# Ordering the QKV projections of a transformer block: values of a chunk inside the next chunk's phase, stores and staged loads placed by modelled times, five block tiles at first, 288 pairs of maxima instead of 296

## The chip, the core and the metric

One core of a Trainium2 chip runs the whole program. The metric is the device time of one launch in microseconds (us), the median of several runs. Engines have short names here: PE is TensorE (matmuls; PEld is its weight load), ACT is ScalarE, DVE is VectorE, POOL is GpSimd, and SP is SyncE, whose queue issues every DMA of the part that changes. Each engine has its own queue of instructions, filled in the order in which the program wrote them; this program writes that order out by hand.

## What is computed

A pre-norm transformer block on one sequence of S = 2048 tokens, width D = 640, 32 heads of 20, in float32:

```python
qkv = layernorm(x) @ wqkv                       # (2048, 640) @ (640, 1920)
p   = softmax(q @ k.T * 20 ** -0.5)             # for each of 32 heads
h   = x + (p @ v) @ wo
out = h + (silu(ln(h) @ w_gate) * (ln(h) @ w_up)) @ w_down     # F = 1728
```

Matmuls on float32 are done as three products of parts: a value is split into a rounded part "hi" and the rest "lo", and hi*hi + lo*hi + hi*lo is summed.

## The kernel before, in words

The program has three stages: the projections (from the start to about 370 us), attention (to about 1520 us), and the output projection and feed-forward part. Only the first stage is rewritten by the change; attention changes by a few instructions.

**Projections.** Tokens come in four chunks of 512 (`NC` = 4). To prepare a chunk its x tiles are loaded (`load_x`), normalised on DVE (`norm`, in small pieces handed out over several steps), and turned by PE (`flip`, five per chunk) into z_hi and z_lo. Then come 10 "blocks" (`query_key`, lines L696 to L705), each the queries or the keys of 128 rows for the chunk's 512 tokens, and 8 "values" (`value`), each 128 tokens by 320 columns. A block is 30 matmuls of half the rows of the array, issued in two halves that run side by side; both kinds are issued at line L498. Before the change the order was fixed per chunk: chunk 0 did ten blocks (the first two together at L715) and then its eight values; chunks 1 and 2 mixed key, query and value and ended with three values; chunk 3 did keys, values, queries. Each entry of this list is a "slot", 18 per chunk, 72 in all.

**A block's way out.** A finished block is split by ACT and DVE or POOL (`keep`: L311, L88, L89) into an "e" tile and stored to DRAM (`qk_d`, line L691) by SP. There are three e tiles in turn: two of their own and one that lies in the values' buffer of attention (the trace calls it `v_stk`; in the last chunk another takes its place, `z_hi`). The flips use the e tiles as scratch too. `keep` doesn't store at once: it puts the store on a list, and the next call of `store`, usually one slot later, issues it (function `store`, L686 to L694). An e tile is written again only when its store has landed.

**Staged maxima.** Attention needs the largest score of each query row before it takes exponentials. Part of these maxima is computed early, inside the projections, to fill PE's gaps: keys and queries of one group of four heads (`g`) and one chunk (`c`) are read back from `qk_d` into a "place" by four DMAs (`stack`, L151, called by `load_items`). Places are quarters of the key buffer of attention (`k_stk`), raw weight tiles that have become free (`raw`), and later the old `z_lo`. For two chunks of keys at once, POOL forms their difference (L376), PE multiplies both (L204), ACT takes a relu (L216) and DVE adds and reduces to the maximum (L210); this makes a "twice" product. A single chunk of keys is folded in half instead (L180, L191, L193), two such products to a "pair". All of it together covers 296 pairs. The rest of the maxima is done in attention (L223, L229), three beside every four scores.

**What sets the order.** A small planner (`Halves`, called `pe`) runs while the program is written: it keeps modelled times of PE's two halves, of ACT, DVE and POOL, and issues a staged product where its model says that its inputs are there and that the engines are free. SP is not modelled before the change: when a group's rows can be loaded is read from a table of slots (`stored_at`), and keys count as loaded 6.5 us (modelled) after the issue.

**Attention** loops over 32 units (a group of four heads by a chunk of queries) with 16 tiles of keys each: four scores (L1225), four exponentials on ACT (L1231), four products with values (L1235).

Of the kernel before, what the change touches and what calls it, by code (L numbers as in the profile page):

```python
# [17 lines left out]
P = 128  # L18
S = 2048
# [28 lines left out]
def tile_block(ctx: ExitStack, tc: tile.TileContext, x, wqkv, wo, wg, wu, wd, out):  # L48
# [111 lines left out]
    def load_queries(u):  # L160

        g, c = divmod(u, NC)
        q = queries[u] = stk.tile([P, 2, CH], F32R, name="q_stk", tag="q_stk", bufs=4)
        stack(q, 0, g, slice(c * CH, (c + 1) * CH))
# [7 lines left out]
    spare = stk.tile([P, 2, CH], F32R, name="q_stk", tag="q_stk", bufs=4)  # L172
# [117 lines left out]
    kept = {}  # L290

    def next_e():
        es.append(es.pop(0))
        if kept.pop(id(es[-1]), 0):
            store()
        return es[-1]

    with tc.tile_pool(name="pa", bufs=2) as pa:
        xs = {}
        zs = {}  # L300
# [3 lines left out]
        def load_x(c):  # L304
            for t in range(c * TPC, (c + 1) * TPC):
                xs[t] = pa.tile([P, D], F32, name="xt", tag="xt", bufs=4)
                nc.sync.dma_start(xs[t], x[t * P : (t + 1) * P, :])
# [9 lines left out]
        slot, returned = [0], []  # L317
# [4 lines left out]
        def stored_at(which, g, c):  # L322

            block = ((g + 1) * GD - 1) // P
            if c == 0:
                return 2 * block + 5
            return 18 * c + 4 + 3 * block + (0 if which else 1)

# [3 lines left out]
        own_places = [None, quarters[0]]  # L332
# [9 lines left out]
        def load_items():  # L342
            for lane, places in lanes:
                while lane:
# [3 lines left out]
                        if slot[0] < LAST_QUARTER or not any(p is k for k in quarters)  # L348
# [4 lines left out]
                    if t is None:  # L353
                        t = raw_tile().rearrange("p a b -> p (a b)")[:, : 2 * CH].rearrange(
                            "p (h n) -> p h n", h=2
                        )
                        fill_ones(t)
                    assert landed[which, g, c] == GD
# [22 lines left out]
        def there(n):  # L381
# [3 lines left out]
            return t is not None and pe.now() >= at + 6.5  # L385
# [3 lines left out]
        def staged_keys(u, kc, ks, q=None, since=0):  # L389
# [18 lines left out]
            def over():  # L408
                for n in ns:
                    users[n] -= 1  # L410
                    if not users[n]:
                        lanes[items[n][6]][1].append(items[n][3])
                if u == 0:
# [23 lines left out]
        for c in (1, 0):  # L437
            for g in range(1, NG, 1 if c else 2):
                if (g, c) == (5, 0):
                    early += third_unit()  # L440
                first = stage(1, g, 1 - c, "plain")
# [17 lines left out]
        def next_pair():  # L459
            load_items()  # L460
            queues = (others, early) if slot[0] >= 18 * (NC - 1) else (early, others)
            return next((queue for queue in queues if queue and queue[0][0]()), None)

        class Halves:
# [5 lines left out]
            def __init__(self):  # L470
                self.t = [0.0, 0.0]
                self.free = dict.fromkeys(("vector", "scalar", "pool"), 0.0)
# [16 lines left out]

            def issue(self, half):  # L490
                job = next(j for j in self.jobs if j["at"][half] < j["n"])
# [66 lines left out]
            def flip(self):  # L558
                for half in range(2):
                    if self.second[half]:  # L560
                        self.finish_second(half)
# [4 lines left out]
                self.use("scalar", 0.48)  # L566
                self.use("pool", 1.3, self.free["scalar"] + 0.1)
                del self.single[0]

# [7 lines left out]
            def wait(self, us):  # L577
                self.t = [self.now() + us] * 2

# [64 lines left out]
        def norm(c):  # L644
# [4 lines left out]
            def apply(t):  # L649
# [5 lines left out]
            zs[c] = (  # L655
                pa.tile([P, ND, CH], F32R, name="z_hi"), pa.tile([P, ND, CH], F32R, name="z_lo")
            )
# [3 lines left out]
                + [(0.6, lambda t=t: apply(t)) for t in range(TPC)]  # L661
            )

        def flip(c, k):
# [7 lines left out]
            split_sbuf(ps, z_hi, z_lo, next_e()[:, 0].bitcast(F32))  # L672
# [10 lines left out]

        stores = []

# [1247 lines left out]
```

## Time and profile before

| | us |
|---|---|
| median of three runs | 2078.84 |
| lowest and highest of them | 2075.09, 2085.61 |
| the profiled execution, whole | 2086.12 |
| its span, first to last instruction | 2084.3 |
| busy in the span: PE | 2037.9 |
| DVE | 1617.8 |
| ACT | 1471.6 |
| POOL | 774.7 |
| mean granted clock of PE | 0.988 of full speed |

The profile is of one execution. "Busy" of PE counts time in which at least one matmul was in the array, so two halves at work and one half at work count the same. A row of the view by windows gives a stretch of the span, its length, the busy time of each engine with the number of its instructions, the mean clock that PE was granted (1.00 is full speed), and the busy share and GB/s of the DMA engines. A row of the chain gives start, length and the piece of work that the end waited for. A row of waits gives the total, the number and the longest.

### The profile page before, as it was taken

The numbers are of one execution on the slowest core, as the hardware profiler recorded it, in microseconds if no ns is written. First come the engines' busy times: TensorE is split into PE (matmuls) and PEld (weight loads), VectorE is DVE, ScalarE is ACT, GpSimd is POOL, SyncE is SP. The second block draws the span as 40 slices with busy tenths as digits, with TensorE's granted clock in tenths as the row PEclk, the third lists the DMA queues.
The fourth block names the chain that finished last, engine by engine and source line by source line (L and its number), as shares of the span: only waits on it lengthen the run. The fifth ranks groups of instructions, "written<-read, shape, count | busy, mean of one in ns | idle before, by whom it ended". The sixth has DMA issues, their size and how long they took to land.

```text
span 2084.3 us, 39077 instructions
## 1 busy us (share of the span) xinstructions
PE 2037.9 (98%) x13656; PEld 1245.0 (60%) x13656; DVE 1617.8 (78%) x3251; ACT 1471.6 (71%) x2941; POOL 774.7 (37%) x1082
## 2 busy tenths in 40 slices
PE   7998999999999999999999999999999999999999
PEld 5887888433333333333333333335588888888888
DVE  6665877888888888888888888885368776676667
ACT  3757888999999989999999999996743222212221
POOL 4433453142425342353432001001145444753556
PEclk9898999899999999999999999999999999999999
DMA  7665665053343432533443113132138755884542
GB/s 223 192 203 150 195 192 170 27 150 111 125 150 121 133 115 97 170 124 126 154 150 120 53 32 95 34 111 64 38 123 293 247 185 173 306 302 156 193 157 95
DMA packets 205292, 305.33 MB, mean 146 GB/s; under 512 B 47640, under 2 KB 82456, under 8 KB 204072
## 3 DMA queue, kind: packets, MB, share of 16 engines
q1 hardware_dynamic: 205000, 302.83, 45.1%
q8 instruction: 109, 1.79, 0.4%
q14 instruction: 87, 0.71, 0.1%
q10 hardware_dynamic: 96, 0.00, 0.0%
HBM read 206.27 MB, written 95.68 MB: 145 GB/s over the span
## 4 chain that ended last, share of the span: by engine, by line
PE 89%; DMA 7%; DVE 1%; issue 1%; POOL 1%; SPq 1%; ACT 1%; POOLq 0%; ACTq 0%; DVEq 0%
PE acc L1235 24%; PE ps_one L1225 16%; PE ps_a L1398 15%; PE ps_max L223 11%; PE ps_b L1492 8%; PE ps_one L498 7%; PE ps_single L204 3%; PE ps_max L963 2%; DMA k_stk<-qk_d 1%; PE ps_b L963 1%; DMA raw<-qk_d 1%; DMA halves<-j_d 1%; DMA q_stk<-qk_d 1%; DMA qk_d<-e 1%; PE ps_single L180 1%
## 5 line engine op out<-in xcount | busy, mean ns | idle before, releaser
L1231 ACT ACTIVATE probs<-ps_one 128x512 f32<-128x512 f32 x2048 | 1057.6, 611 | 66.5 <-PE ps_one L1225 26.3
L229 DVE TENSOR_REDUCE mx<-ps_max 128x1 f32<-128x512 f32 x1456 | 915.7, 684 | 124.9 <-PE ps_max L223 76.4
L1225 PE MATMUL ps_one<-q_stk,k_stk 62*128 62x512 f32 x2048 | 586.5, 432 | 1.0 <-DVE mx L210 1.0
L1235 PE MATMUL acc<-probs,v_stk 128*32 128x512 f32 x4096 | 546.7, 606 | 0.0
L223 PE MATMUL ps_max<-k_stk,q_stk 60*128 60x512 f32 x1456 | 486.1, 440 | 3.4 <-DMA q_stk<-qk_d 3.4
L1225 PEld LDWEIGHTS ps_one<-q_stk,k_stk 62*128 62x128 f32 x2048 | 289.8, 186 | 291.3 <-ACT probs L1231 269.6
L223 PEld LDWEIGHTS ps_max<-k_stk,q_stk 60*128 60x128 f32 x1456 | 241.4, 185 | 169.2 <-DVE mx L229 131.6
L1613 DVE TENSOR_TENSOR tmp<-ps_a,tmp 128x512 f32<-128x512 f32 x208 | 141.1, 689 | 120.2 <-PE ps_a L1398 94.3
L1235 PEld LDWEIGHTS acc<-probs,v_stk 128*32 128x32 f32 x4096 | 80.7, 108 | 180.4 <-issue 172.9
L1492 PE MATMUL ps_b<-halves,yp 128*128 128x320 f32 x1032 | 179.3, 308 | 1.8 <-DMA halves<-j_d 1.2
L1492 PEld LDWEIGHTS ps_b<-halves,yp 128*128 128x128 f32 x1032 | 165.1, 188 | 18.4 <-POOL yp L89 1.5
L1398 PE MATMUL ps_a<-t,units 128*128 128x512 f32 x624 | 162.6, 396 | 0.0
L210 DVE CUSTOM_DVE_ANT_0 q_stk<-ps_single,q_stk 128x512 f32<-128x512 f32 x158 | 105.7, 689 | 50.9 <-ACT q_stk L216 40.1
L1398 PE MATMUL ps_a<-z,units 128*128 128x512 f32 x516 | 133.9, 394 | 0.0
L89 POOL TENSOR_TENSOR yp<-y,yp 128x256 fp32r<-128x256 f32 x96 | 60.3, 628 | 187.8 <-ACT yp L88 187.8
L1398 PEld LDWEIGHTS ps_a<-t,units 128*128 128x128 f32 x624 | 112.6, 188 | 18.6
L240 POOL CAST both<-neg 128x16 fp32r<-128x16 f32 x32 | 6.3, 198 | 309.2 <-DVE neg L236 127.8
L1497 DVE TENSOR_TENSOR h<-ps_b,h 128x320 f32<-128x320 f32 x248 | 109.9, 480 | 7.2 <-PE ps_b L1492 5.7
L498 PE MATMUL ps_one<-z_hi,w_lo 64*128 64x512 f32 x380 | 104.5, 401 | 0.0
L216 ACT ACTIVATE q_stk<-ps_single 128x512 f32<-128x512 f32 x158 | 91.6, 596 | 17.8 <-PE ps_single L204 9.4
L1398 PEld LDWEIGHTS ps_a<-z,units 128*128 128x128 f32 x516 | 93.1, 187 | 16.0
L1270 POOL TENSOR_TENSOR o<-o,rb 128x512 f32<-128x512 f32 x31 | 39.9, 1286 | 164.7 <-DMA q_stk<-qk_d 84.3
(209 smaller groups left out, 3001.4 us busy)
## 6 DMA issues: line engine op xcount, KB each, us to landing
units<-w_d SPq DMA_DIRECT2D x186, 256.0 KB
w_d<-stage SPq DMA_DIRECT2D x106, 256.0 KB
halves<-j_d SPq DMA_DIRECT2D x70, 320.0 KB
k_stk<-qk_d SPq DMA_DIRECT2D x114, 160.0 KB
j_d<-stage SPq DMA_DIRECT2D x42, 320.0 KB
q_stk<-qk_d SPq DMA_DIRECT2D x64, 160.0 KB
k_stk<-qk_d SPq DMA_DIRECT2D x114, 80.0 KB
raw<-qk_d SPq DMA_DIRECT2D x56, 160.0 KB
```

The source lines that it names most:

```text
L210: nc.vector.tensor_tensor_reduce(out=place, in0=pss[1], in1=place, scale=1.0, scalar=LEAST, op0=ALU.add, op1=ALU.max, accum_out=mx[:, b, p ...
L216: nc.scalar.activation(place, pss[0], AF.Relu)
L223: nc.tensor.matmul(ps, queries[u][rows, pair, t * P : (t + 1) * P], keys[u // NC][rows, pair, kc * CH : (kc + 1) * CH], start=True, stop=True,
L229: nc.vector.tensor_reduce(mxs[u][:, b, pair, t, kc : kc + 1], ps, axis=AX.X, op=ALU.max)
L498: product = nc.tensor.matmul(job["ps"][:, :out], lhs, rhs, start=(half == 0 and i == 0), stop=(half == 1 and i == job["n"] - 1),)
L1225: nc.tensor.matmul(ps, keys[u // NC][rows, p, kt * P : (kt + 1) * P], queries[u][rows, p, :], start=True, stop=True,)
L1231: nc.scalar.activation(probs[p][:, b, :], ps, AF.Exp, scale=scale)
L1235: nc.tensor.matmul(acc[32 * j : 32 * j + 32, :], values[u // NC][:, kt, j * VW : j * VW + 32], probs[j // 2][:, j % 2, :], start=(kt == 0) ...
L1398: nc.tensor.matmul(ps.rearrange("p (t n) -> p t n", t=TPC), w[k][:, i], z[k][:, :, j], start=(first and m == 0), stop=(last and m == len(n ...
L1492: nc.tensor.matmul(ps, a, b, start=(n == 0), stop=(n == len(pairs) - 1))
L1497: nc.vector.tensor_tensor(out=h, in0=ps, in1=h, op=ALU.add)
L1613: add = lambda out, ps, x: nc.vector.tensor_tensor(out=out, in0=ps, in1=x, op=ALU.add)
```

## The change

What it does, in the order of the diff:

- The order of slots: ten slots of chunk 0's blocks; then for chunks 1 to 3 a phase of 18 in which two values of the chunk before and two blocks of the chunk alternate, blocks alone at its end; and chunk 3's eight values last. The number of slots stays 72.
- The x tiles of a chunk become one tile with one buffer; flips use the part of it just turned as scratch in place of an e tile.
- e tiles: two query buffers that attention needs only later are lent at first, so there are five, then four, then three; in the last phase two halves of a z_hi tile come and the lent part of the values' buffer goes. `next_e` takes the one whose store is modelled to land first.
- `store` keeps a list with a modelled ready time for each e tile, and `emit_due` issues a store as soon as the modelled time of PE has passed it; SP is modelled with 0.4 us for each DMA, a store as landed 3.0 us and its tile as free 3.5 us after the last of its issues.
- Staged loads are issued when all rows of the group are modelled as landed, and only if SP is modelled to be free within 1 us; keys count as there 4.0 us, queries 4.5 us after the last of the four issues (before: 6.5 us after the first).
- Raw places get their rows of ones by two small DMAs each from the key buffer (`place`) in place of memsets on POOL; two more places come from the x tile in the last phase.
- The last group's first unit (g = 7, c = 0) takes one chunk of keys early (single) in place of two (twice): 288 pairs. Sixteen maxima more are left to attention.
- The last quarters of keys and the last quarter of values are loaded at the end of the stage.

```diff
@@ in_projections
-        return c == 0 and kc <= (2 if g % 2 else 0)
+        return c == 0 and kc <= (1 if g == NG - 1 else 2 if g % 2 else 0)
@@ e tiles and stores
-    kept = {}
+    es += lent
+    stores, e_free, landing = [], {}, {}
+    def emit():
+        job = stores.pop(0)
+        for dst, src, what in job["pieces"]:
+            nc.sync.dma_start(dst, src)
+            pe.sp(job["ready"])
+            for which, n in what:
+                landed[which] += n
+                landing[which] = pe.free["sync"] + 3.0
+        e_free[job["of"]] = pe.free["sync"] + 3.5
+    def emit_due():
+        while stores and stores[0]["ready"] <= pe.now():
+            emit()
+    def store(of, ready, *pieces):
+        stores.append(dict(of=id(of), ready=ready, pieces=pieces))
+    def stored(e):
+        while any(job["of"] == id(e) for job in stores):
+            emit()
+        return e
     def next_e():
-        es.append(es.pop(0))
-        if kept.pop(id(es[-1]), 0):
-            store()
-        return es[-1]
+        waiting = [job["of"] for job in stores]
+        e = min(es, key=lambda e: (id(e) in waiting, e_free.get(id(e), 0.0)))
+        return stored(e)
@@ x tiles and places
-                xs[t] = pa.tile([P, D], F32, name="xt", tag="xt", bufs=4)
+            chunks[c] = pa.tile([P, TPC, D], F32, name="xt", bufs=1)
+        def raw_place():
+            return place(raw_tile().rearrange("p a b -> p (a b)")[:, : 2 * CH])
+        def place(t):
+            ones = k_stk[0][:, 1, S - 2 * CH :]
+            for b in range(2):
+                rows = slice(b * ROW + NPART, (b + 1) * ROW)
+                nc.sync.dma_start(t[rows].bitcast(F32), ones[rows].bitcast(F32))
+            pe.sp(n=2)
+            return t.rearrange("p (h n) -> p h n", h=2)
@@ load_items
-                    if slot[0] < stored_at(which, g, c) or not usable:
+                    if landed[which, g, c] < GD or not usable:
+                        break
+                    if pe.now() < landing[which, g, c] or pe.free["sync"] > pe.now() + 1.0:
                         break
-                        fill_ones(t)
                     stack(t, which, g, slice(c * CH, (c + 1) * CH))
-                    items[lane.pop(0)][3:5] = t, pe.now()
+                    pe.sp(n=4)
+                    items[lane.pop(0)][3:5] = t, pe.free["sync"]
-                if not which or t is None or known is not None or pe.now() < at + 6.5:
+                if not which or t is None or known is not None or pe.now() < at + 4.0:
@@ Halves
+            def sp(self, after=0.0, n=1):
+                self.use("sync", 0.4 * n, after)
             def issue(self, half):
+                emit_due()
@@ flip
-            split_sbuf(ps, z_hi, z_lo, next_e()[:, 0].bitcast(F32))
+            copy = chunks[c][:, :, k * P : (k + 1) * P]
+            split_sbuf(ps, z_hi, z_lo, copy)
@@ the order
+        FIRST = 2 * ND
+        PHASE = 2 * ND + 2 * TPC
+        def begins(c):
+            return FIRST + (c - 1) * PHASE
+        work = [("first", 0), ("none", 0)] + [("block", 0, m) for m in range(2, 2 * ND)]
+        for c in range(1, NC):
+            blocks = [("block", c, m) for m in range(2 * ND)]
+            parts = [("value", c - 1, *divmod(i, 2)) for i in range(2 * TPC)]
+            while parts:
+                work += [parts.pop(0), parts.pop(0), blocks.pop(0), blocks.pop(0)]
+            work += blocks
+        work += [("value", NC - 1, *divmod(i, 2)) for i in range(2 * TPC)]
...
+            if at == 6:
+                own_places.insert(0, raw_place())
+            if at == 9:
+                free_places.extend(raw_place() for _ in range(3))
+            for n in range(1, NC):
+                if at == (2 if n == 1 else begins(n) - 15):
+                    lns = norm(n)
+                if n > 1 and at == begins(n) - 16:
+                    load_x(n)
+            if kind == "first":
+                first_blocks()
+            elif which:
+                (query_key if kind == "block" else value)(c, *which)
+            for n in range(1, NC):
+                if at == (7 if n == 1 else begins(n) - 3):
+                    new_z(n)
+                    flips = [(n, k) for k in range(ND)]
...
+            if at == len(work) - 3:
+                pe.finish_seconds()
+                load_values(0, 0, NT - TPC)
+            if flips:
+                flip(*flips.pop(0))
...
         pe.finish()
-        store()
+        while stores:
+            emit()
         pe.drain()
+        back(False)
+        load_values(0, NT - TPC, NT)
```

More of the change, by code (lines that the diff above doesn't have):

```diff
@@ L170, in load_values, with query_tile @@
         )
-    spare = stk.tile([P, 2, CH], F32R, name="q_stk", tag="q_stk", bufs=4)
+    def query_tile():
+        return stk.tile([P, 2, CH], F32R, name="q_stk", tag="q_stk", bufs=4)
+    lent = [query_tile() for _ in range(2)]
+    spare = query_tile()
     mxs = {u: stk.tile([P, 2, 2, TPC, NC], F32, name=f"mx{u}") for u in range(NU)}
@@ L312, in split_sbuf, with back @@
             split(copy, hi, lo, nc.gpsimd)
-        slot, returned = [0], []
+        slot, returned, coming = [0], [], []
+        def back(now=True):
+            while coming and (not now or coming[0][0] <= pe.now()):
+                assert all(landed[1, 0, c] == GD for c in range(NC))
+                load_keys(0, coming.pop(0)[1])
+                pe.sp(n=4)
         items, users = [], {}
@@ L558, in flip @@
             def flip(self):
-                for half in range(2):
-                    if self.second[half]:
-                        self.finish_second(half)
+                self.finish_seconds()
                 while not self.banks(1):
@@ L682, in flip_tokens @@
             split(ps, *(z[:, :, t * P : (t + 1) * P] for z in zs[0]))
-        stores = []
-        def store(*last, queue=nc.sync):
-            kept.clear()
-            while stores:
-                dst, src, what = stores.pop(0)
-                queue.dma_start(dst, src)
-                if what:
-                    landed[what[0]] += what[1]
-            stores.extend(last)
         def query_key(c, m):
@@ L766, in done @@
                     rows = slice((c * TPC + t) * P, (c * TPC + t + 1) * P)
-                    store((v_d[rows], ev, None))
-                else:
-                    store()
+                    store(ev, free + 0.2, (v_d[rows], ev, ()))
                 return free
```

212 lines of the change are left out of this document (101 added, 111 removed).

## The prediction, made before the changed kernel ran

> **What bounds the kernel now.** I read the page's chain, then busy time and clock by stretches of the first stage, the chain that ended last inside it, SP's own timeline and its waits.
>
> ```profile
> PE 89%; DMA 7%; DVE 1%; issue 1%; POOL 1%; SPq 1%; ACT 1%; POOLq 0%; ACTq 0%; DVEq 0%
> ```
>
> The chain is PE for 89% of the span. DMA is 7% of it, so there is something to gain only where the chain leaves PE. The stretches of the first stage (columns: length, then busy time of PE, PEld, DVE, ACT and POOL, then clock):
>
> ```profile
> 40.00:80.00 40.00, 32.85 (x242) 27.18 (x239) 24.90 (x97) 20.30 (x52) 19.55 (x17) 0.84 0.69 210
> 80.00:140.00 60.00, 59.31 (x583) 54.44 (x583) 44.08 (x212) 44.26 (x122) 22.01 (x17) 1.00 0.62 190
> 140.00:200.00 60.00, 50.42 (x408) 44.36 (x407) 30.42 (x92) 38.20 (x70) 19.09 (x16) 0.86 0.56 169
> 200.00:300.00 100.00, 97.96 (x872) 86.86 (x871) 78.68 (x247) 82.61 (x153) 44.53 (x36) 1.00 0.60 180
> 300.00:320.00 20.00, 17.53 (x183) 17.06 (x181) 13.24 (x45) 14.20 (x28) 10.78 (x10) 0.91 0.72 225
> 320.00:360.00 40.00, 39.85 (x361) 35.63 (x357) 31.62 (x108) 33.73 (x69) 13.78 (x14) 1.00 0.50 159
> 360.00:370.00 10.00, 7.89 (x22) 4.26 (x22) 7.92 (x24) 7.45 (x13) 1.27 (x1) 0.69 0.42 129
> ```
>
> From 80 to 140, 200 to 300 and 320 to 360 us PE is full and at full clock. It loses time in four stretches. I add idle time and the part of the length lost to the clock (an upper bound, since the two can overlap): 40 to 80: 7.15 + 0.16 x 40 = 13.6 us; 140 to 200: 9.6 + 0.14 x 60 = 18.0; 300 to 320: 2.5 + 0.09 x 20 = 4.3; 360 to 370: 2.1 + 0.31 x 10 = 5.2. Together 41 us. What the first two wait for is in the chain, and in SP's timeline at the same places:
>
> ```profile
> 17.91 7.10 PE ps_one L715 x30
> ...
> 42.30 5.41 DMA qk_d<-v_stk
> 49.24 4.54 DMA k_stk<-qk_d
> ...
> 63.39 0.96 POOL raw L140
> 64.37 4.95 DMA raw<-qk_d
> 69.34 4.28 DMA qk_d<-e
> 73.73 0.61 ACT e L311
> ...
> 134.98 5.59 DMA raw<-qk_d
> 140.67 6.44 DMA k_stk<-qk_d
> 147.12 4.40 DMA qk_d<-e
> 151.68 0.61 ACT e L311
> ...
> 169.10 5.34 DMA raw<-qk_d
> 174.46 5.26 DMA qk_d<-v_stk
> 179.83 0.61 ACT v_stk L311
> ...
> 369.70 0.79 PE ps_one L1225
> ```
>
> ```profile
> 39.00 1.67 SPq L151 DMA_DIRECT2D raw<-qk_d  x4
> 42.30 1.45 SPq L691 DMA_DIRECT2D qk_d<-v_stk  x3
> 173.07 10.18 SPq L691 DMA_DIRECT2D qk_d<-v_stk  x4
> ```
>
> Three times the same pattern ends in a block that can't leave its bank: ACT waits for an e tile (73.73, 151.68, 179.83) whose store landed only then, and the store stood on SP behind staged loads, which themselves waited for a memset on POOL or a place. At 39.00 a staged load of four DMAs goes out ahead of the store at 42.30.
>
> **The change part by part.** A block is 30 half-array products, two halves at once: 15 x 7.10/30 = 3.55 us. Three e tiles hold 10.7 us of blocks, five 17.8.
>
> (1) *Stores by ready time, five tiles, flips without e tiles, ones by DMA instead of memset; the 40 to 80 stretch.* All four act on the pattern at 42 to 74. A tile's way, 0.6 us on ACT, about as much on DVE, and 4.3 to 5.4 of landing, is some 7 us if SP takes the store at once; five tiles leave 10.8 us to spare. Bounds 0 to 13.6; the stretch 200 to 300 keeps 2 us of idle time in 100 with three tiles, so nearly all could go. I take 10, since the first maxima still hang on loads here. Next to be late is the staged keys of the first groups.
>
> (2) *The same, and chunk 1's blocks from slot 12 instead of 18; the 140 to 200 stretch.* The stall is the same, and DVE has only 30.4 of 60 us of work there, because twice products need chunk 1's blocks; these now come earlier. Bounds 0 to 18.0; I take 13.
>
> (3) *300 to 320:* 0 to 4.3, I take 2. *360 to 370* is the drain: staged products left after the last block, PE waiting for DVE. Chunk 3's values, with one ACT operation each, stand there now. Between 5 us less and, if maxima pile up, as much more; I take 0.
>
> (4) *Eight pairs fewer.*
>
> ```profile
> L210 DVE CUSTOM_DVE_ANT_0 q_stk<-ps_single,q_stk 128x512 f32<-128x512 f32 x158 | 105.7, 689 | 50.9 <-ACT q_stk L216 40.1 <-PE ps_single L204 6.4 <-PE ps_one L498 2.3
> L89 POOL TENSOR_TENSOR e<-e 128x512 fp32r<-128x512 f32 x22 | 28.7, 1306 | 51.4 <-ACT e L88 33.0 <-DMA k_stk<-qk_d 8.5 <-issue 4.3
> L193 DVE CUSTOM_DVE_ANT_0 q_stk<-ps_single,q_stk 128x256 f32<-128x256 f32 x96 | 36.1, 418 | 15.7 <-ACT q_stk L191 15.1
> 1360.00:1380.00 20.00, 20.00 (x147) 7.81 (x140) 17.91 (x30) 19.51 (x39) 1.71 (x3) 1.00 0.57 170
> 1440.00:1460.00 20.00, 20.00 (x132) 9.17 (x128) 7.33 (x26) 15.78 (x33) 0.74 (x1) 1.00 0.34 109
> ```
>
> Sixteen twice products become 16 folded ones: on PE 16 half products less, 16/2 x 0.237 = -1.9 us; on DVE 16 x (0.689 - 0.418) = -4.3. PE is the bound, so -2 (bounds -4.3 and 0). In attention 16 maxima more: PE is full with them (1360) and without (1440), so 16 x 0.237 = +3.8; 0 if ACT, at 19.5 of 20, carries that stretch anyway. I take 3.8.
>
> (5) *Shorter due times.* Keys now count as there 4.0 us after the last issue. The chain shows 4.54, 4.95, 5.59, 6.44 and 5.34 from there, mean 5.4. If PE or POOL stands at its wait for the difference in each of the 23 staged groups (seven, seven, four, one and four), that is 32 us; the other end is 0, as SP, PE and POOL may all run behind the model together. What PE waited for staged keys before:
>
> ```profile
> PE ps_single L204 <- POOL k_stk L376: 1.2, 1, 1.2
> PE ps_single L180 <- POOL raw L376: 0.8, 1, 0.8
> SPq L691 <- POOL e L89: 22.9, 8, 7.3
> SPq L633 <- POOL w_lo L89: 2.4, 2, 1.8
> ```
>
> That is 2 us in all; the model lagged by enough then. With less margin I take 4, nearer to this row than to the other end, because real PE comes to each product later than modelled. The Trainium skill, page "DMA: Bandwidth & Descriptors", in its anatomy of one DMA, fits about 2.0 us plus the bytes at 436 GB/s for one path, which would give an estimated 2.75 us for 320 KB. This trace disagrees, with 4.28 to 5.41 us for stores; by the page the term would be 0 and the sum 4 us lower.
>
> (6) *Ones by DMA:* 12 DMAs on SP, 12 x 0.39 (42.30's row has 1.45 for three, so 0.48 at most) = 5 to 6 us of SP, beside PE's work; they wait for raw tiles that POOL still reads (2.4 us in the row above), with stores behind them. Five tiles cover that: 0; without cover 2.4 at two places. *The next x* is loaded right after the last flip, whose scratch POOL still reads; SP stands there for two operations of ACT and one of POOL, 2 x 0.6 + 1.3 = 2.5 us, for chunks 2 and 3, with stores and loads behind. Covered by free e tiles: 0; without, 5. Values later, one x tile, and the split last loads change no count of PE's work: 0, the loads having 16 tiles of keys to land in.
>
> Sum: -10 - 13 - 2 + 0 - 2 + 3.8 + 4 = -19 us. The profiled execution took 2086.1 and becomes 2067; it stands 7.3 above the median of the runs shown, so the median goes from 2078.8 to 2060.
>
> **The rivals.**
>
> *The stall moves to staged loads* (no change). Term (5) at 28 of its 32 instead of 4: -19 + 24 = +5, 2084; half of that with maxima left over for the end (18 twice products at the 0.69 of L210, 12 us): 2079 - 19 + 12 + 12 = 2084 again. For it: the five landings. Against it: only 2 us of such waits now.
>
> *SP stands at stores that aren't ready* (slower). A store is issued when the model says that POOL has finished, a slot earlier than now; if POOL is later, SP waits with all loads behind it. The rows: 10.18 us for four DMAs at 173.07, and 22.9 us of waiting for POOL's e already. A stretch like 140 to 200 costs 18 us. If (2) gains nothing and one more such stretch comes in the last phases: -10 - 2 + 3.8 + 4 + 18 = +14, 2093. It turns slower from the point where SP's wait outlasts the free tiles, 10.8 us with five, but 10.7 - 7 = 3.7 with the three of the later phases. The Trainium skill, "TensorE: Matmul & The Clock Gate", Part 1, adds that an idle window of about 3.4 us halves the clock until a busy window has passed. The trace agrees: 0.84 and 0.86 in the two stalled stretches, 1.00 in the full ones.
>
> *All of it goes:* 41 of stalls less, -2 and +3.8: 2040.
>
> **How the numbers follow.** No change that a measurement of this kernel can tell is within 0.5%, 10.4 us. The forecast with its terms between 10 and 38 us of gain, 2040 to 2068: 0.58; more than that: 0.04. The no-change rival: 0.20. The slower one: 0.18. So faster 0.62, same 0.20, slower 0.18. The range 2040 to 2091 leaves out 0.04 below and most of the upper half of the slower case.
>
> **What would show it.** Right: the first score (L1225), at 369.70 in the chain above, near 347 us (25 us of stalls and 2 of work less, 4 of term 5 more); clock 1.00 between 40 and 80 and where chunk 1's blocks run; no chain piece in which a store of an e tile ends behind staged loads; ACT's wait for e near 0; PE's wait for staged keys a few us; L210 in 208 and L193 in 160 products; maxima in attention 1472. Wrong: PE waiting for L376 or for landings by tens of us, SP held at L691 by POOL for longer than the 22.9 us now, or a drain of over 10 us between the last value and the first score.

## The result and the profile after

The changed kernel takes 2065.3 us (median of six runs, 2057.0 to 2066.9), the one before 2084.6 in the same comparison (2075.1 to 2088.1). The ratio is 0.991 with a 95% interval of 0.9883 to 0.9936: faster by 19 us or 0.9%. The forecast was a gain of 19 us, from 2079 to 2060; both medians came out some 5 us higher.

The page's chain of the changed kernel, and its first stage by the same stretches as before the change (columns again: length, then busy PE, PEld, DVE, ACT, POOL, then clock):

```profile
span 2064.9 us, 39006 instructions
PE 91%; DMA 4%; DVE 3%; issue 1%; SPq 1%; ACT 0%; POOL 0%; POOLq 0%; DVEq 0%; ACTq 0%
```

```profile
40.00:80.00 40.00, 36.53 (x297) 30.36 (x295) 26.48 (x105) 27.54 (x70) 20.22 (x16) 0.96 0.70 210
80.00:140.00 60.00, 56.43 (x529) 51.70 (x526) 50.71 (x221) 44.54 (x119) 20.45 (x16) 1.00 0.75 233
140.00:200.00 60.00, 56.82 (x525) 51.13 (x527) 48.45 (x149) 46.64 (x88) 24.76 (x19) 1.00 0.64 198
200.00:300.00 100.00, 94.22 (x856) 86.18 (x854) 69.31 (x224) 79.90 (x155) 41.76 (x36) 0.97 0.56 166
300.00:320.00 20.00, 20.00 (x180) 18.02 (x178) 16.32 (x51) 17.65 (x33) 9.92 (x10) 1.00 0.62 179
```

DMA's share of the chain falls from 7 to 4%. By the measure of the prediction (idle time plus the length lost to the clock) the old stalls shrink from 13.6 to 5.1 us (40 to 80) and from 18.0 to 3.2 (140 to 200). Two stretches that had been full now lose time: 80 to 140 goes from 0.7 to 3.6, and 200 to 300 from 2.0 to 8.8.

The first score of attention, by its matmul line, marks the end of the first stage. The kernel before, the changed kernel, and the changed kernel in another execution (`e12_changed_again`), a line each; behind the three durations (ns) stand the first and the last start:

```profile
L1225 PE MATMUL ps_one<-q_stk,k_stk x2048: 383/397/792, 369.7 to 1516.5; 62*128 62x512 f32 x187
```

```profile
L1290 PE MATMUL ps_one<-q_stk,k_stk x2048: 383/397/792, 345.2 to 1497.4; 62*128 62x512 f32 x187
```

```profile
L1290 PE MATMUL ps_one<-q_stk,k_stk x2048: 383/397/794, 339.2 to 1488.9; 62*128 62x512 f32 x187
```

The first stage ends 24.5 us earlier. What follows takes 2064.9 - 345.2 = 1719.7 us where it took 2084.3 - 369.7 = 1714.6, so attention and what comes after it give 5.1 back in this pair of executions. The third line is a caution: one and the same program ended its first stage 6 us earlier in another execution. Below, a first score counts as moved only beyond 6 us, and the verdicts go by the ratios.

### The profile page after: what moved, and what is told of

It reads as the page before. It is cut to its first block, busy times and chain, and to the rows that moved or that the text cites. A ratio compares the mean times of both kernels' runs of the same rounds, so it can differ in the third digit from the quotient of the medians.

```text
span 2064.9 us, 39006 instructions
## 1 busy us (share of the span) xinstructions
PE 2024.8 (98%) x13656; PEld 1237.5 (60%) x13656; DVE 1627.8 (79%) x3267; ACT 1466.0 (71%) x2941; POOL 762.4 (37%) x1069
## 4 chain that ended last, share of the span: by engine, by line
PE 91%; DMA 4%; DVE 3%; issue 1%; SPq 1%; ACT 0%; POOL 0%; POOLq 0%; DVEq 0%; ACTq 0%
PE acc L1300 24%; PE ps_one L1290 16%; PE ps_a L1463 15%; PE ps_max L227 12%; PE ps_one L543 8%; PE ps_b L1557 8%; PE ps_single L208 2%; PE ps_max L1028 2%; PE ps_b L1028 2%; DMA halves<-j_d 1%; PE ps_single L184 1%; DMA k_stk<-qk_d 1%; DMA q_stk<-qk_d 1%; DMA raw<-qk_d 0%; DVE xt L699 0%
## 5 line engine op out<-in xcount | busy, mean ns | idle before, releaser
L1296 ACT ACTIVATE probs<-ps_one 128x512 f32<-128x512 f32 x2048 | 1058.4, 613 | 70.6 <-PE ps_one L1290 30.4
L233 DVE TENSOR_REDUCE mx<-ps_max 128x1 f32<-128x512 f32 x1472 | 925.6, 684 | 128.2 <-PE ps_max L227 79.1
L227 PE MATMUL ps_max<-k_stk,q_stk 60*128 60x512 f32 x1472 | 492.4, 440 | 4.9 <-DVE mx L233 2.5
L214 DVE CUSTOM_DVE_ANT_0 q_stk<-ps_single,q_stk 128x512 f32<-128x512 f32 x138 | 93.0, 689 | 30.9 <-ACT q_stk L220 24.6
L88 ACT ACTIVATE yp<-tmp 128x512 fp32r<-128x512 f32 x40 | 25.3, 632 | 103.1 <-POOL tmp L1550 103.1
L543 PE MATMUL ps_one<-z_hi,w_lo 64*128 64x512 f32 x380 | 98.0, 395 | 0.0
L543 PE MATMUL ps_one<-z_lo,w_hi 64*128 64x512 f32 x380 | 93.8, 396 | 2.6 <-POOL z_lo L89 2.6
```

The lines of the kernel that those rows point to most:

```text
L214: nc.vector.tensor_tensor_reduce(out=place, in0=pss[1], in1=place, scale=1.0, scalar=LEAST, op0=ALU.add, op1=ALU.max, accum_out=mx[:, b, p ...
L227: nc.tensor.matmul(ps, queries[u][rows, pair, t * P : (t + 1) * P], keys[u // NC][rows, pair, kc * CH : (kc + 1) * CH], start=True, stop=True,
L233: nc.vector.tensor_reduce(mxs[u][:, b, pair, t, kc : kc + 1], ps, axis=AX.X, op=ALU.max)
L543: product = nc.tensor.matmul(job["ps"][:, :out], lhs, rhs, start=(half == 0 and i == 0), stop=(half == 1 and i == job["n"] - 1),)
L1296: nc.scalar.activation(probs[p][:, b, :], ps, AF.Exp, scale=scale)
```

## The experiments

| run | first score, us | median, us | ratio to the kernel before (95%) |
|---|---|---|---|
| changed kernel | 345.2 | 2065.3 | 0.991 (0.9883 to 0.9936) |
| e12_changed_again | 339.2 | 2061.9 | 0.9907 (0.9887 to 0.9926) |
| e1_three_tiles | 345.1 | 2058.1 | 0.9903 (0.9874 to 0.9931) |
| e2_late_stores | 338.4 | 2062.8 | 0.9919 (0.9891 to 0.9948) |
| e5_tiles_as_before | 343.9 | 2062.9 | 0.9923 (0.9897 to 0.995) |
| e3_old_order | 343.0 | 2071.1 | 0.9971 (0.9953 to 0.9988) |
| e4_296_pairs | 352.1 | 2064.9 | 0.9929 (0.9905 to 0.9952) |
| e6_greedy_loads | 348.9 | 2069.9 | 0.9952 (0.9934 to 0.997) |
| e7_memset_ones | 351.3 | 2068.8 | 0.9949 (0.9932 to 0.9967) |
| e8_long_due | 338.8 | 2056.4 | 0.989 (0.9865 to 0.9915) |
| e11_long_due_stores_first | 336.6 | 2058.6 | 0.9891 (0.987 to 0.9912) |
| e9_load_rule_alone | 353.9 | 2072.2 | 0.9957 (0.9942 to 0.9973) |
| e10_no_load_rule | 365.2 | 2094.8 | 1.0062 (1.0039 to 1.0084) |

The rows come from several comparisons, each with its own runs of the kernel before. So the price of a part is given below as the difference of two ratios times 2080 us, and not as the difference of two medians.

### The block tiles: three instead of five, late stores, and both with the flips

```diff
-    es += lent
```

> The changed kernel with three e tiles until the last phase instead of five, four and three; stores, loads and order stay timed by the model. Theory of the prediction (term 1 is a matter of tiles and of stores behind loads together): part of the stall of chunk 0's blocks returns, ACT waits for stores of e tiles by 4 us or more, the first score comes at 350 to 355 us instead of 345.2, the whole is 5 to 10 us above the changed kernel's 2065. Rival (the timing of the stores alone removed the stall, three tiles are enough as 10.7 us of blocks cover 7 us of way): first score within 2 us of 345, the whole within 3 us of 2065.

```diff
-        stores.append(dict(of=id(of), ready=ready, pieces=pieces))
+        stores.append(dict(of=id(of), ready=ready + 3.5, pieces=pieces))
```

> The changed kernel with every store modelled as ready 3.5 us later, so that it is issued about one slot late as before; tiles and order stay. Theory (stores stand behind staged loads): the first score comes 3 to 10 us later than 345.2, and the staged keys with it, since every group is loaded a slot later. Rival (the tiles alone removed the stall; four or five of them have 3.5 us to spare): within 2 us.

Both undo their part without any loss: 0.9903 and 0.9919. With three tiles ACT waits for no store of an e tile, where the theory expected 4 us or more. With late stores the first score comes 6.8 us earlier and not later; that is outside what the rival allowed too, but only 0.8 us from the changed kernel's other execution. So neither theory holds. To see whether tiles, stores and flips merely cover for each other, all three went back together:

```diff
-    es += lent
...
-        stores.append(dict(of=id(of), ready=ready, pieces=pieces))
+        stores.append(dict(of=id(of), ready=ready + 3.5, pieces=pieces))
...
-            copy = chunks[c][:, :, k * P : (k + 1) * P]
+            e = next_e()
+            e_free[id(e)] = pe.free["pool"] + 0.2
+            copy = e[:, 0].bitcast(F32).rearrange("p (t n) -> p t n", t=TPC)
```

> Everything about a block's way out as before at once: three e tiles, flips that use them as scratch, stores a slot late; order, load rule and ones by DMA stay changed. Theory (tiles and stores are one cause, and any one of them alone hides the others): ACT waits for stores of e tiles by 8 us or more again, the first score at 355 us or later, the whole at 2072 or more. Rival (the rule for staged loads and the ones are what ended the stalls): first score within 4 us of 345, the whole within 4 us of 2065.

ACT's waits for stores of e tiles, and two stretches:

```profile
ACT e L337 <- DMA qk_d<-e: 6.8, 2, 3.9
ACT v_stk L337 <- DMA qk_d<-v_stk: 1.6, 1, 1.6
```

```profile
40.00:80.00 40.00, 36.42 (x268) 29.96 (x265) 18.18 (x64) 20.90 (x48) 19.90 (x16) 0.87 0.76 242
...
200.00:300.00 100.00, 98.53 (x912) 89.09 (x909) 77.08 (x248) 86.82 (x169) 46.88 (x40) 1.00 0.58 175
```

ACT's waits of before come back in part, 8.4 us of 22.3 (the four rows of the kernel before: 8.1, 6.0, 5.0 and 3.2), and the early stretch loses 8.8 us instead of 5.1. But the first score stays at 343.9 and the ratio at 0.9923, and 200 to 300 loses only 1.5. So the tiles do what they were meant to do at their place, and it decides nothing at the end of the stage in this order.

### The order of slots

```diff
-            return FIRST + (c - 1) * PHASE
+            return c * PHASE
...
+        work += [("value", 0, *divmod(i, 2)) for i in range(2 * TPC)]
         for c in range(1, NC):
-            blocks = [("block", c, m) for m in range(2 * ND)]
-            parts = [("value", c - 1, *divmod(i, 2)) for i in range(2 * TPC)]
-            while parts:
-                work += [parts.pop(0), parts.pop(0), blocks.pop(0), blocks.pop(0)]
-            work += blocks
-        work += [("value", NC - 1, *divmod(i, 2)) for i in range(2 * TPC)]
+            ks = [("block", c, 2 * i) for i in range(ND)]
+            qs = [("block", c, 2 * i + 1) for i in range(ND)]
+            parts = [("value", c, *divmod(i, 2)) for i in range(2 * TPC)]
+            if c < NC - 1:
+                work += [a for some in zip(ks, qs, parts) for a in some] + parts[ND:]
+            else:
+                work += ks + parts + qs
...
-                if at == (7 if n == 1 else begins(n) - 3):
+                if at == (7 if n == 1 else begins(n) - 6):
...
-            if at == begins(NC - 1) + 15:
+            if at == begins(NC - 1) + 3:
...
-            for u, when in enumerate((5, begins(1) + 14, begins(2) + 14)):
+            for u, when in enumerate((5, begins(1) + 6, begins(2) + 6)):
```

> The changed kernel with the order of slots of before: chunk 0's values behind its blocks, key, query and value mixed in chunks 1 and 2, keys, values, queries in chunk 3; stores and loads stay timed by the model, with five tiles. Theory (term 2 needs chunk 1's blocks early): DVE is light again somewhere between 100 and 200 us, the first score comes 8 to 13 us later than 345.2, the whole is at 2072 to 2079. Rival (the timing of stores and the tiles are the whole gain, order none): first score within 3 us of 345, the whole within 4 us of 2065.

The whole loses two thirds of the gain, 0.9971, but not for the reason expected. The first score is at 343.0, and the stretch that term 2 was about is fuller than in the changed kernel:

```profile
140.00:200.00 60.00, 58.84 (x554) 53.46 (x553) 47.58 (x148) 50.73 (x95) 25.63 (x20) 1.00 0.68 210
```

Inside the stage this kernel has a stall of its own, 7.6 us in which PE waits for a difference of POOL between 290 and 300, but its first score is no later for it. The loss that shows comes right after the first score. PE and SP of this run in order of time (start, length):

```profile
340.92 1.31 PE L543 MATMUL ps_one<-z_hi,w_lo 64*128 64x512 f32 x5
342.96 0.50 PE L1292 MATMUL ps_one<-q_stk,k_stk 62*128 62x512 f32 x1 [0.74 <-ACT e L338]
352.48 0.76 PE L227 MATMUL ps_max<-k_stk,q_stk 60*128 60x512 f32 x1 [9.01 <-DMA k_stk<-qk_d]
```

```profile
340.88 4.84 SPq L301 DMA_DIRECT2D qk_d<-e  x5
345.82 1.93 SPq L151 DMA_DIRECT2D k_stk<-qk_d  x4
```

With queries as the last blocks, the stores of their e tiles stand on SP at 340.88 ahead of the last load of keys, and PE waits 9.0 us for it. In the changed kernel values come last and no such wait exists. The stretch of the hand-over to attention, in this run and in the changed kernel:

```profile
340.00:370.00 30.00, 20.25 (x115) 9.42 (x112) 16.12 (x35) 18.22 (x37) 2.11 (x2) 0.77 0.30 76
```

```profile
340.00:370.00 30.00, 28.99 (x191) 14.13 (x188) 21.76 (x42) 24.34 (x50) 0.15 (x1) 0.94 0.15 50
```

By the measure of the prediction they lose 16.7 and 2.8 us. The 14 us between them are about what the ratios say that the old order costs here, 13 us. So this loss lies at the hand-over to attention, not in the middle. It is not in the order alone: `e9_load_rule_alone` below has the same order, its last load of keys goes out at 324.65, and PE has no such wait. The code before loaded its last keys at 355.17, ahead of the last stores, and paid a drain of staged products there.

### Staged loads: the rule, and the rows of ones

```diff
-                    if pe.now() < landing[which, g, c] or pe.free["sync"] > pe.now() + 1.0:
-                        break
```

> The changed kernel without the two conditions on staged loads (rows modelled as landed, SP modelled as free within 1 us): a load is issued as soon as the stores of its rows have been issued and a place is free. Theory (SP stands at loads whose rows have not landed, with stores behind): SP's waits at L151 grow by 10 us or more, the first score 5 to 15 us later than 345.2, the whole at 2070 to 2080. Rival (five tiles cover it; loads that go sooner only help): first score within 3 us of 345 or earlier.

The ratio rises to 0.9952. SP, and what PE waited for:

```profile
37.59 2.67 SPq L301 DMA_DIRECT2D qk_d<-v_stk  x3
42.53 1.43 SPq L151 DMA_DIRECT2D k_stk<-qk_d  x4
44.06 1.27 SPq L301 DMA_DIRECT2D qk_d<-q_stk  x3
48.47 2.96 SPq L151 DMA_DIRECT2D k_stk<-qk_d  x8
51.48 2.35 SPq L151 DMA_DIRECT2D q_stk<-qk_d  x4
```

```profile
PE ps_single L184 <- DMA raw<-qk_d: 14.5, 1, 14.5
```

The load at 42.53 and the one at 48.47 each go out when a store of just before has landed (37.59 + 4.9 and 44.06 + 4.4), so SP stands idle with the next store behind. A staged product that the model had put early then holds PE for 14.5 us. (The profile puts this wait down to a load into `raw`; the product itself reads `k_stk` and `q_stk`, and the load into `q_stk` goes out at 51.48.) It is one long stall, not many, and by the ratios some 9 us of it are left at the end. The forecast of 10 us or more in SP's waits at L151 did not come: the five largest rows of L151 sum to 51.0 us, where they sum to 57.0 in the changed kernel.

```diff
-            ones = k_stk[0][:, 1, S - 2 * CH :]
-            for b in range(2):
-                rows = slice(b * ROW + NPART, (b + 1) * ROW)
-                nc.sync.dma_start(t[rows].bitcast(F32), ones[rows].bitcast(F32))
...
+            fill_ones(t)
```

> The changed kernel with the rows of ones of new places written by memsets on POOL again instead of by DMA (two of about 1 us for each of six places). Theory: the memsets stand on POOL between the differences and behind the raw weights' splits, in the chain at 60 to 64 us before the change; the stretch 40 to 80 loses 2 to 5 us, the whole 0 to 5 us above 2065. Rival (POOL, at about a third of its time, has room): within 1 us at the first score.

```profile
40.00:80.00 40.00, 35.98 (x291) 30.00 (x289) 24.85 (x103) 28.36 (x73) 28.57 (x24) 0.96 0.64 198
```

POOL rises from 20.2 to 28.6 us of this stretch. PE loses only half a us more in it. But PE's longest wait for a difference of POOL in this run is 5.2 us, and the stretch from 200 to 300 us loses 16.3 us where the changed kernel loses 8.8. So the cost appears later: 0.9949, first score at 351.3. That is some 8 us by the ratios, but the interval of 0.9932 to 0.9967 clears only that of the changed kernel's second measurement, and not that of the first (up to 0.9936).

### The load rule with the other large parts as before

Here the order of slots, the three tiles, the flips through them, the late stores and the memsets all went back (the edits of `e5_tiles_as_before`, `e3_old_order` and `e7_memset_ones` together), once with the load rule and once without. The short due times, the 288 pairs, the choice of an e tile by its modelled landing and the one x tile of a chunk stay in both.

> The changed kernel with the order of slots, the three tiles, flips through them, late stores and memsets of before all at once; of the large parts only the rule for staged loads (rows modelled as landed, SP modelled as free) and the short due times stay, with 288 pairs. Theory now (no part about tiles or stores matters; loads that go when their rows have landed and SP is free are what ended the stalls, and the order is worth the 6 us at the hand-over): first score at 345 to 352 us, the whole at 2068 to 2076. Rival (each part alone covers for the others, so that with all of them gone the stalls are back): first score at 360 us or later, the whole at 2077 or more.

> The same as e9_load_rule_alone without the load rule: a load goes as soon as the stores of its rows are issued and a place is free. Theory: stalls of 5 us and more return, as SP stands at loads before the stores, first score 8 to 20 us later than in e9_load_rule_alone. Rival (the rule is worth only the 4 us that it was worth in the changed kernel): within 5 us of it.

With the rule, ACT's waits for stores and SP's waits for landings of rows:

```profile
ACT e L337 <- DMA qk_d<-e: 7.2, 2, 5.6
```

```profile
SPq L151 <- DMA qk_d<-e: 11.3, 7, 4.0
```

Without it, the same two views and then its stretches from 40 to 200 us:

```profile
ACT e L337 <- DMA qk_d<-e: 20.6, 5, 10.5
```

```profile
SPq L151 <- DMA qk_d<-e: 19.1, 7, 5.8
```

```profile
40.00:80.00 40.00, 29.66 (x187) 23.13 (x183) 13.86 (x42) 13.55 (x32) 21.62 (x19) 0.84 0.57 179
80.00:140.00 60.00, 59.32 (x531) 56.64 (x531) 39.26 (x198) 42.11 (x120) 16.99 (x14) 0.88 0.53 165
140.00:200.00 60.00, 56.39 (x507) 49.57 (x507) 43.33 (x148) 45.69 (x93) 23.84 (x19) 0.97 0.59 185
```

The same stretches with the rule:

```profile
40.00:80.00 40.00, 34.16 (x266) 26.73 (x264) 21.64 (x76) 22.70 (x54) 26.53 (x24) 0.96 0.63 197
80.00:140.00 60.00, 58.77 (x595) 57.04 (x594) 47.06 (x226) 41.97 (x121) 16.70 (x13) 1.00 0.69 211
140.00:200.00 60.00, 57.99 (x528) 51.70 (x526) 44.13 (x135) 49.69 (x93) 24.76 (x20) 1.00 0.61 187
```

These two kernels differ in two lines, and by 22.6 us: 0.9957 against 1.0062. Half of it, 11.3 us, is there at the first score. The other half comes after it:

```profile
PE ps_max L227 <- DMA k_stk<-qk_d: 9.2, 1, 9.2
```

It is the wait of `e3_old_order`, for keys that are loaded behind the last stores. The kernel with the rule doesn't have it here, but `e3_old_order`, which keeps the rule, does; so this half isn't shown to be the rule's. The first half is the pattern of the prediction. By its measure the three stretches lose 16.7 + 7.9 + 5.4 = 30.0 us without the rule and 7.4 + 1.2 + 2.0 = 10.6 with it; the kernel before lost 32.3, the changed kernel 11.9. ACT's 20.6 us of waits for stores of e tiles are nearly the 22.3 of the kernel before. So the pattern is real, and in these two kernels the rule for loads ends it, most of it between 40 and 80 us; the large stall from 140 to 200 (18.0 us before) comes back only as 5.4 there, and as 7.9 from 80 to 140. Added to the changed kernel without the rule (`e6_greedy_loads`), the same two lines are worth some 9 us; that the five tiles, early stores and order absorb the rest there is the likely reading, but no run takes them apart. With the rule and none of the other large parts, about half of the gain is left. The rule is compared with no rule here, while the kernel before had a table of slots, which lies between; the rule put into the kernel before alone was not run.

### Due times

```diff
-                if not which or t is None or known is not None or pe.now() < at + 4.0:
+                if not which or t is None or known is not None or pe.now() < at + 5.4:
...
-            return t is not None and pe.now() >= at + 4.5
+            return t is not None and pe.now() >= at + 5.9
```

> The changed kernel with staged keys counted as there 5.4 us and queries 5.9 us after the last issue instead of 4.0 and 4.5. Theory (term 5): PE's waits for staged keys (7.7 us in the changed kernel: POOL raw 2.7 and 1.8, DMA k_stk 2.4, q_stk 0.8) fall below 3 us and the first score comes 3 to 6 us earlier than 345.2. Rival (products start later and the maxima left over at the end take it back): first score at 345 or later.

What PE waited for in the changed kernel: three rows of staged products, and in the second row a block whose z_lo POOL had not made yet:

```profile
PE ps_single L184 <- POOL raw L413: 2.7, 1, 2.7
PE ps_one L543 <- POOL z_lo L89: 2.6, 1, 2.6
PE ps_single L184 <- DMA k_stk<-qk_d: 2.4, 1, 2.4
PE ps_single L208 <- POOL raw L413: 1.8, 1, 1.8
```

The second row belongs to them. In the chain that ended last, z_lo stands on POOL behind the difference of a staged group, and PE behind z_lo:

```profile
239.87 1.26 POOL k_stk L413
241.13 1.23 POOL z_lo L89
242.41 0.86 PE ps_one L543 x4
```

With the longer times, 200 to 300 us:

```profile
200.00:300.00 100.00, 99.46 (x903) 89.69 (x902) 79.21 (x254) 88.16 (x171) 44.79 (x38) 1.00 0.59 182
```

PE is full there, with 0.5 us lost instead of 8.8 (6.9 in the other execution of the changed kernel), and both waits of that stretch, 2.7 and 2.6 us, are gone. But PE's waits for staged rows and their differences were to fall from 7.7 below 3 us, and they are still 6.0: 3.0 at L184 between 40 and 50, 3.0 at L208 at 167. The stretch from 80 to 140 still loses 4.0. The first score, 338.8, lies where the changed kernel can also come out, and 0.989 isn't separated from 0.991.

```diff
+                        while stores:
+                            emit()
                         load_w(loaded)
```

> The changed kernel with the longer due times of e8_long_due (5.4 and 5.9 us) and with the waiting stores issued ahead of each load of raw weights, behind which the first stores stood on SP until 32 us. Theory: PE's gap at 40 to 50 us (3.2 us) closes at least half, the first score at 334 to 338 us, the whole 8 to 13 us below the changed kernel of the same chip. Rival (the gap only moves to the first staged loads): as e8_long_due, 338 to 339 us.

The first stores do leave SP earlier, but PE still idles for 10 - 6.61 = 3.4 us between 40 and 50, where it idles for 3.2 in the changed kernel: the gap stays, as the rival said. What PE waits for in it, in the changed kernel, is staged rows, 2.4 us for keys and 0.8 for queries:

```profile
47.00 0.46 PE L184 MATMUL ps_single<-k_stk,q_stk 60*128 60x512 f32 x1 [2.38 <-DMA k_stk<-qk_d]
48.25 0.47 PE L184 MATMUL ps_single<-k_stk,q_stk 60*128 60x512 f32 x1 [0.79 <-DMA q_stk<-qk_d]
```

DVE is busy for 9.36 of these 10 us, since the normalisation of chunk 1 now stands in slots 2 to 6, between the low parts of blocks and weights:

```profile
40.00:50.00 10.00, 6.83 (x55) 5.34 (x53) 9.36 (x21) 3.39 (x8) 4.38 (x4) 0.96 0.72 229
```

```profile
40.17 0.60 DVE q_stk L89
...
43.83 4.60 DVE xt L699 x3
```

It can reach PE through SP: the low part at 40.17 ends at 40.77, its store goes out at 40.80 and the load of the queries behind it at 42.70. A busy DVE alone doesn't cost PE this time: in `e5_tiles_as_before` DVE is busy for 9.77 of the same 10 us and PE for 9.35. How much of the gap is the normalisation's is not shown.

`e11_long_due_stores_first` and `e8_long_due` have the lowest ratios of the table together with `e1_three_tiles`. Neither is separated from the changed kernel; the measured median of `e11_long_due_stores_first` is 3.3 us below that of `e12_changed_again` on the same chip, with overlapping intervals. That a version beats the changed kernel is not shown.

> The changed kernel itself, beside e11_long_due_stores_first on the same chip. All theories: first score within 3 us of 345.2, 0.989 to 0.993 of the time before.

The ratio came out as expected; the first score moved by 6.0 us where 3 were allowed.

### 296 pairs

```diff
-        return c == 0 and kc <= (1 if g == NG - 1 else 2 if g % 2 else 0)
+        return c == 0 and kc <= (2 if g % 2 else 0)
...
-                if (g, c) == (NG - 1, 0):
-                    early += staged_keys(g * NC, 1, [stage(1, g, 1)], stage(0, g, 0))
-                    continue
```

> The changed kernel with 296 pairs: the last group's first unit takes two chunks of keys early again. Theory (term 4): the stage ends 2 to 5 us later, attention is 3.8 us shorter, the whole within 2 us of 2065. Rival (attention carries 16 maxima for nothing because ACT sets its pace): the stage 2 to 5 us later and the whole by as much, 2067 to 2070.

The stage ends at 352.1 and what follows takes 2064.4 - 352.1 = 1712.3 us, 7.4 less than in the changed kernel's first profile. The other kernels with 288 pairs take 1715.0 (`e8_long_due`) to 1718.8 us from there, leaving out the two with the wait at the hand-over, so 2.7 to 7.4 is what eight pairs cost behind the first score. The whole is the same, 0.9929. So the theory holds in kind: the stage is longer, attention shorter. The size of either term is not settled better than that, and the stage's 6.9 us hardly exceed the 6 between two executions. Part of attention's term is a new wait in the changed kernel; its last maxima meet the statistics of the next projection on DVE, and the stretch where they do shows it:

```profile
1430.89 1.25 PE L227 MATMUL ps_max<-k_stk,q_stk 60*128 60x512 f32 x2 [1.35 <-DVE mx L233]
```

```profile
1420.00:1440.00 20.00, 18.54 (x108) 7.62 (x106) 12.03 (x33) 13.10 (x27) 0.98 (x2) 0.91 0.30 99
```

## Why the prediction was right, and where its reasons were not

The size and the sign are right, and so is where the largest part of the time went: out of the two stalled stretches of the first stage. By steps, with the measured figures of the profile after:

- **(1) 40 to 80 us**, predicted 10 us less: 8.5. **(2) 140 to 200**, predicted 13 less: 14.8. The sizes are right, since the loss was read off as idle time plus clock at those places. The reason for taking 10 of 13.6 in (1) held too: "the first maxima still hang on loads here". Of the 5.1 us that are left, 3.2 are PE's waits for the first staged rows.
- **The cause inside (1) fell in part.** The step said that four parts act on one pattern, and put tiles and stores first. Tiles, late stores and flips undone, alone (`e1_three_tiles`, `e2_late_stores`) or together (`e5_tiles_as_before`), cost nothing that can be measured in the whole. The part that the runs single out is the rule for staged loads: with the other large parts undone, 40 to 200 us loses 10.6 us with it and 30.0 without, and the first score moves by 11.3 (`e9_load_rule_alone` against `e10_no_load_rule`). The prediction had the right row, the load at 39.00 ahead of the store at 42.30, and didn't name the rule as the term.
- **The cause inside (2) fell.** "Chunk 1's blocks from slot 12" was to feed DVE. With the old order 140 to 200 is full all the same, and DVE has 47.6 us of work there in place of 30.4, so the early blocks aren't needed for it. That DVE was light because of the stall, and not the reverse, fits this. What ended the stall at this place is not shown by itself.
- **(3)**, predicted 2 + 0: 300 to 320 lost its 4.3, and the drain of 5.2 us at 360 to 370 is gone, since the first score follows the last value's evacuation by 0.6 us. The term was 7.5 us too small. What removed the drain is not shown: the old order under the new code has none before its first score either (0.7 us, `e3_old_order`), but waits 9.0 us just behind it.
- **(4)** attention predicted at +3.8: +5.1 in the two profiles, with 1.4 us of it a wait for DVE; single executions give 2.7 to 7.4 for it (`e4_296_pairs`). On the first stage -2 was predicted for PE's work; what eight pairs move there is up to 6.9 us, but that is hardly above the 6 us between two executions.
- **(5) Shorter due times**, predicted +4: between 200 and 300 us 6.8 us more are lost than before. There PE waits 2.7 us for a difference and 2.6 for the z_lo behind one, and `e8_long_due` takes both away, with 8.3 of the 8.8 us lost. So the mechanism was right, and the size 2.8 us too small. In the whole the longer times gain some 4 us, which isn't separated from none. The Trainium skill's fit for one DMA ("DMA: Bandwidth & Descriptors", anatomy of one DMA) would have made the term 0. The page gives it for DMAs that GpSimd issues, while SP issues these; with a margin of 4.0 us for them PE does wait here.
- **(6) Ones by DMA**, predicted 0 (its 12 x 0.39 us on SP are 4.7, a little under the 5 to 6 given): the memsets would cost some 8 us by the ratios, barely clear of the spread (`e7_memset_ones`). The squeezed normalisation wasn't priced; whether it costs PE anything is not shown.
- **80 to 140 us**, without a term: 2.9 us more are lost than before. PE stands there for 3.6 us (1.57, 1.50 and 0.51) at products that wait for DVE's maxima, and not for rows; `e8_long_due` still loses 4.0 there. The row of these waits, for the whole stage:

```profile
PE ps_single L184 <- DVE mx L197: 3.9, 4, 1.6
```

So the sum came out within 1 us partly by luck. Term (3) was 7.5 us too small as a gain. Against it stand costs that were too small or missing: 2.8 us in (5), 2.9 between 80 and 140 and 1.3 in attention, 7.0 together.

Of the signs that were named, the counts came out (208 twice products, 160 folded ones, 1472 maxima in attention), the first score came at 345.2 for 347, and ACT waits for no store of an e tile. The clock between 40 and 80 is 0.96 and not 1.00, and in one place the chain still has a store of an e tile behind staged loads, at 235.74. The rival "the stall moves to staged loads" was present at about a third of its price: PE's waits for staged rows, for their differences and for the z_lo behind one are 10.3 us, where it took 28. "SP stands at stores that aren't ready" got no worse: SP's waits at stores for POOL were 38.9 us before and 32.0 after for the same two rows, while its waits for ACT's values rose from 7.3 to 14.1:

```profile
SPq L301 <- POOL v_stk L89: 17.1, 3, 7.4
...
SPq L301 <- POOL e L89: 14.9, 7, 4.8
```

The row for v_stk before the change, 16.0 us, was not shown in the prediction; it stands here:

```profile
SPq L691 <- POOL v_stk L89: 16.0, 4, 7.1
```

## What to carry to other kernels

When one queue issues both stores and loads, ask of each load whether its rows have landed at the moment of issue: in this kernel a load that had to wait held the stores behind it on SP's queue, and the engines that needed the stores' tiles stood still in a place where no load is seen (20.6 us of ACT's waits without the rule). Parts of a change that act on the same stall can cover for each other, so undoing one at a time may show little; take all the others away, and then try one with and without. Look at the seam between two stages for itself: a first instruction of the next stage can come early and the work behind it stand still (here at 343.0 us, and then for 9.0), because a load was left on the queue behind the last stores.

## What was not expected of the hardware

The same program ended its first stage at 345.2 us in one execution and 339.2 in another, with mean clocks of 0.994 and 0.996, on a whole of 2066.9 and 2058.9 us. In a stage whose order was fixed to tenths of a us by a model, single executions differ by more than most of its terms, and only whole-kernel ratios over several runs, or a stretch that is full in one kernel and not in the other, can carry a verdict of that size.
